# Attention with beacons and a low-rank mixer on one core: q of the third and fourth pair on SyncE's queue, w1's first quarter ahead of v's second half, U and V rounded later, and the first mixing's blocks side by side

## The chip, the cores and the metric

The kernel runs on one core of one Trainium2 chip. The metric is device time in microseconds (us) of one execution. Three runs of the kernel before gave 350.47, 351.5 and 351.79 us, so the median is 351.5 us.

## What is computed

Eight batches of eight heads attend over 576 tokens of 64 numbers. Sixteen beacon keys and values stand ahead of the tokens and are seen by every query; the tokens are causal. The attention output, as a 576 x 512 matrix x for each batch, goes through a mixer: a low-rank mixing along the tokens, and then a feed-forward layer with 2048 inner columns.

```python
scores = (q @ k_all.T) / 8            # k_all = beacons, then keys; causal on the keys
a = softmax(scores); x = a @ v_all    # 8 heads side by side: 576 x 512
u = x + ((x.T @ U) @ V).T             # U: 576 x 32, V: 32 x 576
out = u + relu(u @ w_ch1) @ w_ch2     # w_ch1: 512 x 2048, w_ch2: 2048 x 512
```

Everything comes in as float32; the kernel computes in float16 and accumulates in float32.

## The kernel before, in words

Two heads make a pair, four pairs make a batch. For each pair, k and q come in with the tokens on the partitions. TensorE transposes them (`tps`), VectorE copies the transposes to `kT` and `qT` (L310). TensorE makes the scores (`sps`, L342 and L350 for the first pairs), ScalarE takes their exponentials to `expt` (L356), and TensorE multiplies these with v (`po`, L399, one `av` unit of 15 matmuls per head). VectorE normalises the result into `xb` (L407, L408). When a batch is done its mixing runs, and then the feed-forward products: `gps` (L536, with w1) and `cps` (L562, with w2). All is written out in one order for every engine; each engine takes its instructions in that order, and the order is what the change edits.

What matters here is batch 0, the first 30 us. It is loaded through three queues.

- SyncE (SP) and ScalarE start q and k of pair 0 in float32 into `stq` and `stk` (`load_first`). After that SP loads q of pair 1 in float32 (`build_masks`, L127), released by a small write of VectorE to `stq` (L126). `regroup` (L270) then rounds such a q to float16 on VectorE, with the two heads side by side (`pr`), so that TensorE transposes it in 6 instructions (L277). A pair that is loaded as float16 is transposed in 12 instructions, head by head (L283).
- GpSimd (POOL) starts everything else, and its DMAs round to float16 on the way: k of pairs 1 and 2, q of pair 2, v's beacons, v of heads 0 to 3 (five DMAs, `v_tokens`, L220), k and q of pair 3, v of heads 4 to 7, and the first quarter of w1 (`emit_w1(0)`, L191). Then POOL rounds U (L178) and V (L179), which SP has loaded in float32 into `small` (`small_loads`), and goes on with batch 1: k and q of its heads 0 to 3, k's beacons, w1's second quarter, and so on.
- V is wanted four times, on partitions 0, 32, 64 and 96 (`Vsb`), and its last 80 columns in a block matrix (`Vend`). SP copies them there from partition 0 by seven small DMAs (L183, L184).

The first mixing, of batch 0, goes in two halves of two 128-column blocks (`first_mix`). `head` makes x.T U for two blocks: 5 matmuls, one per token tile, each with 32 output partitions and 256 columns (`qtp`, L491). VectorE rounds it to `qts` (L494). `begin` puts x transposed into PSUM (L415), `rest` adds V's product with 2 matmuls of 496 columns and 2 of 80 (L508), all four with 32 input partitions, and ScalarE and VectorE copy the sums to `uT`. The later mixings (`mix_units`, L436 and L461) do four blocks at once, each on its own 32 columns or rows of TensorE.

The order around the change is: `kt` and `qt` of pairs 2 and 3 with the scores of pairs 1 to 3 between them, `av` of pairs 0 and 1, `av` of the first head of pair 2, `head(0, 2)`, `av` of the second head, `begin`, `rest(0, 2)`, both heads of pair 3, `begin` for block 2, four products with w1 (`part(D0, 2)`, `part(D1, 2)`), `head(2, 2)`, `begin` for block 3, two more, `rest(2, 2)`, the transposes of batch 1's first pair (`qkT_of(4)`), and the feed-forward products of the first 512 rows.

Of the kernel before, what the change touches and what calls it, by code (L numbers as in the profile page):

```python
# [11 lines left out]
F32 = mybir.dt.float32  # L12
# [6 lines left out]
P = 128  # L19
# [11 lines left out]
def kernel(  # L31
# [13 lines left out]
    nc = tc.nc  # L45
    B, H, S, D = q.shape
    Nb = beacon_k.shape[2]
    DM = H * D
    R = moe_U.shape[1]
# [13 lines left out]
    NT = NC  # L63
# [58 lines left out]
    def build_masks():  # L122
        make_identity(nc, ident)
        nc.vector.memset(bigmask[:, 0, P - Nb : P], F16_MAX)
        nc.vector.tensor_copy(out=identb, in_=ident)
        nc.vector.memset(first[1][0:1, 2, 0:1], 0.0)  # L126
        token_load(nc.sync, q[0], first[1], SETS[1])  # L127
        make_upper_triangular(nc, mask, val=F16_MAX, diag=True)
        token_load(nc.gpsimd, k[0], Ls[0][0][0], SETS[1])
        nc.vector.tensor_copy(out=bigmask[:, 0, 0 : P - Nb], in_=mask[:, Nb:P])  # L130
        nc.vector.tensor_copy(out=bigmask[:, 1, :], in_=mask)
        for i in range(2):
            nc.vector.tensor_scalar(
                out=negmask[:, i, :], in0=bigmask[:, i, :], scalar1=1.0, scalar2=NEG,
                op0=ALU.is_lt, op1=ALU.mult,
            )
        prs[0] = [None, regroup(first, 0, 1, V, act_copy)]
# [26 lines left out]
    def small_loads():  # L164

        f = utp.tile([P, NT * R + S], F32, name="small", tag="ut")
        nc.vector.memset(f[0:1, 0:1], 0.0)
        uf, vf = f[:, 0 : NT * R].rearrange("p (j r) -> p j r", r=R), f[0:R, NT * R :]
        nc.sync.dma_start(out=uf[: nq[0], 0, :], in_=moe_U[0 : nq[0], :])
        nc.sync.dma_start(  # L170
            out=uf[:, 1 : NT - 1, :], in_=moe_U[q0[1] : QM, :].rearrange("(j p) r -> p j r", p=P)
        )
        nc.sync.dma_start(out=uf[:NL, NT - 1, :], in_=moe_U[QM:S, :])
        nc.sync.dma_start(out=vf, in_=moe_V)

        def cast():
            for rr, jj in ((nq[0], slice(0, 1)), (P, slice(1, NT - 1)), (NL, slice(NT - 1, NT))):
                nc.gpsimd.tensor_copy(out=Usb[:rr, jj, :], in_=uf[:rr, jj, :])  # L178
            nc.gpsimd.tensor_copy(out=Vsb[0:R, :], in_=vf)  # L179
            for cc in range(NCC):  # L180
                rs = ds(R * cc, R)
                if cc:
                    nc.sync.dma_start(out=Vsb[rs, :], in_=Vsb[0:R, :])  # L183
                nc.sync.dma_start(out=Vend[rs, cc, :], in_=Vsb[0:R, QM:S])  # L184

        return cast

# [16 lines left out]
    def token_load(eng, src, dst, hs):  # L204
        eng.dma_start(out=dst[0:TP, hs, :], in_=src[hs].rearrange("h (p j) d -> p h (j d)", j=TJ))  # L205
# [277 lines left out]
    def first_mix(xb):  # L483

        qts = outp.tile([P, DM], F16, name="qfirst", tag="ob")
        cell = {}

        def head(c0, n):
            qtp = pst([R, P * n], F32, name="qtp")
            for j in range(NT):  # L490
                nc.tensor.matmul(  # L491
                    qtp, Usb[: nq[j], j, :], xb[: nq[j], j, ds(P * c0, P * n)], start=(j == 0), stop=(j == NT - 1)
                )
            nc.vector.tensor_copy(out=qts[0:R, ds(P * c0, P * n)], in_=qtp)  # L494
            emptying(qtp)

        def begin(c0, cs, n=2):
            for cc in cs:
                cell[cc] = pst([P, QM], F32, name="ups")
                x_into(xb, cell[cc], cc, list(range(NT - 1)), 0, True)  # L500
                if cc == c0:
                    cell["end"] = pst([P, n, NL], F32, name="uend")
                x_into(xb, cell["end"][:, cc - c0, :], cc, [NT - 1], QM, cc == c0)

        def rest(c0, n, copies, end):
            for at in (0, QM):
                for i in range(n):
                    nc.tensor.matmul(  # L508
                        cell["end"][:, i, :] if at else cell[c0 + i], qts[0:R, ts(c0 + i, P)],
                        Vsb[0:R, at : S if at else QM], start=False, stop=True, skip_group_check=True,  # L510
                    )
# [161 lines left out]
    def load_first():  # L673

        kf = gtp.tile([P, 2, TJ * D], F32, name="stk", tag="gT")
        qf = gtp.tile([P, 4, TJ * D], F32, name="stq", tag="gT")
        first.extend([kf, qf])
        for src, dst in ((q[0], qf), (k[0], kf)):
            for eng, h in ((nc.sync, 0), (nc.scalar, 1)):
                token_load(eng, src, dst, slice(h, h + 1))  # L680
        Ls[0] = qk_tiles()
        key_beacons(nc.gpsimd, beacon_k[0], Ls[0][0][0], ALLH)
        nc.scalar.activation(out=warm, in_=ones, func=AF.Exp)

    def act_copy(out, in_):
        nc.scalar.activation(out=out, in_=in_, func=AF.Copy)
# [125 lines left out]
    with tc.manual_schedule(engines={ENG.PE, ENG.Activation, ENG.DVE, ENG.SP, ENG.Pool}):  # L812
        load_first()
        build_masks()
        for c in (2, 3):
            for src, dst in zip((k[0], q[0]), Ls[0][0]):
                token_load(nc.gpsimd, src, dst, SETS[c])
            if c == 2:
                v_beacon(beacon_v[0], vss[0])
                v_tokens(v[0], vss[0], HALVES[0])  # L820
        prs[0][0] = regroup(first, 0, 0, V, act_copy, beacons=False)
        idle(IDLE[0], plain)
        t0, sc = qkT_of(0), scores_of(0)
        t0[0]()
        idle(IDLE[4], ident)
        t0[1]()
        sc[0](IDLE[1], gs=[1, 0])
        prs[1] = [None, regroup(first, 1, 1, V)]
        for u in qkT_of(1):
            u()  # L830
        clear()
        cast = small_loads()
        sc[1]([3, 2], False)
        sc = scores_of(1)
        sc[0](IDLE[2])
# [19 lines left out]
        for p in range(2):  # L855
            qt, kt = qkT_of(p + 2)
            kt()
            sc[1]([3, 2], False)
            qt()
            av = av_of(p)  # L860
            av[0]()
            mask_head = sc[3]
            sc = scores_of(p + 2)
            if p:
                mask_head(0)
            sc[0](0, av[1])
            if p:
                mask_head(1)
# [252 lines left out]
```

## Time and profile before

| what | us |
|---|---|
| median of three runs | 351.5 |
| lowest and highest | 350.47, 351.79 |
| the profiled execution | 349.7 |
| its span, first to last instruction | 348.0 |
| TensorE (PE) busy in the span | 341.3 |
| VectorE, ScalarE, GpSimd busy | 189.7, 163.6, 97.8 |

The profiled execution took 1.7 us more than its span, which lies ahead of and behind the span. It is 1.8 us below the median. In the lists below, a row of the timeline gives the start in us, the time in us, the engine, the line, the operation, what is written and read with its shape, and the count of instructions that were merged; in square brackets stands the idle time of the engine before them and what ended it. A row of the chain of work gives start, time, engine, what is made and the line. A row of the DMA view gives what is written and read, the queue, the count, the KB of one DMA and the us from issue to landing. A row of the view by stretches gives the stretch, its length, the busy time of each engine, the granted clock of TensorE, the mean share of the 16 DMA engines and the GB/s that they wrote.

### The profile page before, as it was taken

The numbers are of one execution on the slowest core, as the hardware profiler recorded it, in microseconds if no ns is written. First come the engines' busy times: TensorE is split into PE (matmuls) and PEld (weight loads), VectorE is DVE, ScalarE is ACT, GpSimd is POOL, SyncE is SP. The second block draws the span as 40 slices with busy tenths as digits, with TensorE's granted clock in tenths as the row PEclk, the third lists the DMA queues.
The fourth block names the chain that finished last, engine by engine and source line by source line (L and its number), as shares of the span: only waits on it lengthen the run. The fifth ranks groups of instructions, "written<-read, shape, count | busy, mean of one in ns | idle before, by whom it ended". The sixth has DMA issues, their size and how long they took to land.

```text
span 348.0 us, 7791 instructions
## 1 busy us (share of the span) xinstructions
PE 341.3 (98%) x3084; PEld 173.2 (50%) x3084; DVE 189.7 (55%) x493; ACT 163.6 (47%) x358; POOL 97.8 (28%) x137
## 2 busy tenths in 40 slices
PE   8899999999999999999999999999999999999995
PEld 4565565455554455444554445455445444444443
DVE  6676965788875553554465556535655542323311
ACT  6957851578723664167615752494434203202300
POOL 8966714544506457303930130000000000000000
PEclk9999999999999999999999999999999999999999
DMA  9999999999999999991999697713122314013011
GB/s 166 135 186 170 169 200 171 216 148 154 128 142 145 167 133 132 154 213 14 146 139 237 64 117 123 184 38 68 62 75 47 69 62 121 2 60 106 17 66 64
DMA packets 146635, 41.88 MB, mean 120 GB/s; under 512 B 131488, under 2 KB 142080, under 8 KB 146592
## 3 DMA queue, kind: packets, MB, share of 16 engines
q0 software_dynamic: 87440, 18.18, 68.2%
q1 hardware_dynamic: 58928, 22.84, 36.0%
q8 instruction: 26, 0.43, 0.5%
q10 hardware_dynamic: 224, 0.30, 0.2%
q14 instruction: 17, 0.14, 0.1%
HBM read 37.37 MB, written 9.44 MB: 134 GB/s over the span
## 4 chain that ended last, share of the span: by engine, by line
PE 93%; POOL 2%; DMA 2%; issue 1%; DVE 1%; ACT 1%; POOLq 0%
PE gps L536 36%; PE cps L562 35%; PE po L399 8%; PE sps L384 6%; DMA st<-in_q_dram 2%; PE tps L277 1%; PE sps L350 1%; POOL vs L220 1%; PE cph L588 1%; PE qtp L436 1%; POOL st L205 1%; PE tps L283 1%; PE ups L461 1%; PE ups L415 1%; ACT expt L356 0%
## 5 line engine op out<-in xcount | busy, mean ns | idle before, releaser
L536 PE MATMUL gps<-uT,w 128*128 128x512 f16 x576 | 136.0, 379 | 0.1
L562 PE MATMUL cps<-w,gT 128*128 128x512 f16 x560 | 130.9, 379 | 0.0
L390 ACT ACTIVATE expt<-sps 128x496 f16<-128x496 f32 x192 | 82.5, 534 | 71.5 <-PE sps L384 71.5
L549 ACT ACTIVATE gT<-gps 128x512 f16<-128x512 f32 x86 | 50.9, 622 | 78.8 <-PE gps L536 78.6
L536 PEld LDWEIGHTS <-w 128*128 128x128 f16 x576 | 51.8, 98 | 58.0 <-issue 2.4
L562 PEld LDWEIGHTS <-gT 128*128 128x128 f16 x560 | 50.8, 98 | 58.9 <-issue 6.2
L551 DVE TENSOR_SCALAR gT<-gps 128x512 f16<-128x512 f32 x58 | 40.0, 690 | 41.9 <-PE gps L536 40.5
L575 DVE TENSOR_TENSOR ob<-cps,ut 128x512 f32<-128x512 f32 x31 | 21.4, 691 | 48.3 <-PE cps L562 47.5
L220 POOL DMA_DIRECT2D vs<-in_v_dram x50 | 39.6, 810 | 17.1 <-PE gps L536 5.8
L399 PEld LDWEIGHTS <-expt 128*128 128x128 f16 (+1 forms) x960 | 36.2, 98 | 12.7 <-issue 0.8
L399 PE MATMUL po<-vs,expt 128*128 128x65 f16 (+1 forms) x960 | 38.9, 194 | 0.0
L408 DVE TENSOR_TENSOR xb<-po,rec 128x320 f16<-128x320 f32 x64 | 31.5, 492 | 2.2
L326 DVE TENSOR_TENSOR expt<-expt,bigmask 128x512 f16<-128x512 f16 x58 | 24.1, 416 | 6.7 <-ACT expt L390 6.7
L356 ACT ACTIVATE expt<-sps 128x496 f16<-128x496 f32 (+2 forms) x64 | 27.1, 584 | 0.9 <-PE sps L350 0.8
L407 DVE RECIPROCAL rec<-po 128x5 f32<-128x5 f32 x64 | 12.1, 188 | 27.0 <-PE po L399 26.8
L384 PE MATMUL sps<-qT,kT 64*128 64x80 f16 (+4 forms) x288 | 23.3, 281 | 0.1
L202 POOL DMA_DIRECT2D vs<-in_beacon_v_dram x8 | 4.3, 536 | 57.8 <-PE po L399 57.7
L384 PEld LDWEIGHTS <-kT 64*128 64x128 f16 x288 | 9.9, 94 | 18.3 <-issue 14.8
L651 POOL DMA_DIRECT2D st<-in_q_dram x20 | 16.9, 863 | 6.6 <-DMA vs<-in_v_dram 2.7
L651 POOL DMA_DIRECT2D st<-in_k_dram x20 | 17.0, 883 | 3.4 <-DMA st<-in_q_dram 3.4
L448 DVE TENSOR_TENSOR uT<-ups,uT 128x496 f16<-128x496 f32 x24 | 14.5, 667 | 5.0 <-PE ups L461 5.0
L310 DVE COPY qT<-tps 128x576 f16<-128x576 f16 (+1 forms) x16 | 11.8, 736 | 4.6 <-PE tps L283 2.8
(98 smaller groups left out, 161.9 us busy)
## 6 DMA issues: line engine op xcount, KB each, us to landing
out_dram<-ob SPq DMA_DIRECT2D x35, 256.0 KB, 2.3
vs<-in_v_dram POOLq DMA_DIRECT2D x18, 128.0 KB, 6.9
w<-in_moe_w_ch_dram POOLq DMA_DIRECT2D x4, 512.0 KB, 6.1
w<-in_moe_w_ch_dram POOLq DMA_DIRECT2D x2, 1024.0 KB, 13.6
st<-in_k_dram POOLq DMA_DIRECT2D x12, 128.0 KB, 8.6
st<-in_q_dram POOLq DMA_DIRECT2D x12, 128.0 KB, 9.6
st<-in_k_dram POOLq DMA_DIRECT2D x2, 576.0 KB, 13.2
st<-in_q_dram POOLq DMA_DIRECT2D x2, 576.0 KB, 16.1
```

The lines of the kernel that those rows point to most:

```text
L220: nc.gpsimd.dma_start(out=dst[a : a + nq[j], j, :, :], in_=src[hs, ds(q0[j], nq[j]), :].rearrange("h p d -> p h d"))
L326: nc.vector.tensor_tensor(out=e4, in0=e4, in1=bigmask, op=ALU.min)
L356: nc.scalar.activation(out=ex[i][:, ds(SLOT * g, gw[g])], in_=ps[g, i][:, 0 : gw[g]], func=AF.Exp, scale=scale)
L384: nc.tensor.matmul(ps[p, g, i][:, ds(o, w)], kT[hp, c, ds(P * ch, P)], qT[hp, c, ds(qa, w)], start=True, stop=True,)
L390: nc.scalar.activation(out=at[p][3][i][:, ds(SLOT * g, gw[g])], in_=ps[p, g, i][:, 0 : gw[g]], func=AF.Exp, scale=scale)
L399: nc.tensor.matmul(po[:, j, :], ex[0 : nk[c], ds(blk[(c, j)], P)], vs[0 : nk[c], ds(c * H * E + h * E, E)], start=(c == 0), stop=(c == j),)
L408: nc.vector.tensor_tensor(out=xb[:, :, ds(h * D, D)], in0=po[:, :, 0:D], in1=r.broadcast_to([P, NT, D]), op=ALU.mult)
L536: nc.tensor.matmul(g[:, 0:n], w1[:, cc, ts(dc, P)], uT[:, cc, ds(t0, n)], start=(cc == 0), stop=(cc == NCC - 1))
L549: nc.scalar.activation(out=gT["t"][:, dc, 0:n], in_=g[:, 0:n], func=AF.Relu)
L551: nc.vector.tensor_scalar_max(out=gT["t"][:, dc, 0:n], in0=g[:, 0:n], scalar1=0.0)
L562: nc.tensor.matmul(ps[:m, :], gT["t"][:, dc, ds(P * i, m)], w2[:, dc, :], start=(dc == 0), stop=turned and dc == NDC - 1, skip_group_check ...
L651: nc.gpsimd.dma_start(out=dst[a : m[j], j, :, :], in_=src[:, ds(q0[j], nq[j]), :].rearrange("h p d -> p h d"))
```

## The change

Four things are changed, all within batch 0.

1. q of pairs 2 and 3 no longer comes through POOL's queue as float16. SP loads both in float32 into a larger `stq`, right behind q of pair 1, and VectorE rounds them (`regroup` into `pr`): pair 2 behind the clearing of `expt`, pair 3 between the k and q transposes of pair 2. TensorE transposes each with 6 instructions in place of 12.
2. On POOL, w1's first quarter is started ahead of v of heads 4 to 7. The rounding of U and V is moved behind the first three loads of batch 1.
3. U and V are loaded earlier on SP's queue (`small_loads` stands ahead of pair 1's transposes), and V comes twice, on partitions 0 and 32. POOL rounds both and writes two of Vend's four blocks; SP's copies fall from seven to four.
4. In the first mixing, `head` makes 10 matmuls of 128 columns, the two blocks on their own 32 columns of TensorE, and `rest` adds V's product from two groups of 32 rows; the 80-column products go over 64 rows with `Vend`. `begin(2, (2,))` now stands between the two heads of pair 3.

```diff
 (build_masks)
-        nc.vector.memset(first[1][0:1, 2, 0:1], 0.0)
-        token_load(nc.sync, q[0], first[1], SETS[1])
+        load_q(1)
 (small_loads)
-        uf, vf = ..., f[0:R, NT * R :]
+        uf, vf = ..., f[0 : 2 * R, NT * R :]
-        nc.sync.dma_start(out=vf, in_=moe_V)
+        for i in range(2):
+            nc.sync.dma_start(out=vf[ds(R * i, R), :], in_=moe_V)
 (cast)
-            nc.gpsimd.tensor_copy(out=Vsb[0:R, :], in_=vf)
+            nc.gpsimd.tensor_copy(out=Vsb[0 : 2 * R, :], in_=vf)
             for cc in range(NCC):
                 rs = ds(R * cc, R)
-                if cc:
+                if cc > 1:
                     nc.sync.dma_start(out=Vsb[rs, :], in_=Vsb[0:R, :])
-                nc.sync.dma_start(out=Vend[rs, cc, :], in_=Vsb[0:R, QM:S])
+                    nc.sync.dma_start(out=Vend[rs, cc, :], in_=Vsb[0:R, QM:S])
+                else:
+                    nc.gpsimd.tensor_copy(out=Vend[rs, cc, :], in_=vf[rs, QM:S])
 (first_mix, head)
-            qtp = pst([R, P * n], F32, name="qtp")
+            qtp = pst([R * n, P], F32, name="qtp")
             for j in range(NT):
-                nc.tensor.matmul(
-                    qtp, Usb[: nq[j], j, :], xb[: nq[j], j, ds(P * c0, P * n)], start=(j == 0), stop=(j == NT - 1)
-                )
+                for i in range(n):
+                    nc.tensor.matmul(
+                        qtp[ds(R * i, R), :], Usb[: nq[j], j, :], xb[: nq[j], j, ts(c0 + i, P)],
+                        start=(j == 0), stop=(j == NT - 1), skip_group_check=True, tile_position=(0, R * i),
+                    )
 (first_mix, rest)
-            for at in (0, QM):
-                for i in range(n):
-                    nc.tensor.matmul(
-                        cell["end"][:, i, :] if at else cell[c0 + i], qts[0:R, ts(c0 + i, P)],
-                        Vsb[0:R, at : S if at else QM], start=False, stop=True, skip_group_check=True,
-                    )
+            for i in range(n):
+                nc.tensor.matmul(
+                    cell[c0 + i], qts[ds(R * i, R), ts(c0, P)], Vsb[ds(R * i, R), 0:QM],
+                    start=False, stop=True, skip_group_check=True,
+                )
+            for i in range(n):
+                nc.tensor.matmul(
+                    cell["end"][:, i, :], qts[0 : R * n, ts(c0, P)], Vend[0 : R * n, i, :],
+                    start=False, stop=True, skip_group_check=True,
+                )
 (load_first)
-        qf = gtp.tile([P, 4, TJ * D], F32, name="stq", tag="gT")
+        qf = gtp.tile([P, H, TJ * D], F32, name="stq", tag="gT")
+    def load_q(*cs):
+        for c in cs:
+            nc.vector.memset(first[1][0:1, 2 * c, 0:1], 0.0)
+        for c in cs:
+            token_load(nc.sync, q[0], first[1], SETS[c])
 (the order)
         for c in (2, 3):
-            for src, dst in zip((k[0], q[0]), Ls[0][0]):
-                token_load(nc.gpsimd, src, dst, SETS[c])
+            token_load(nc.gpsimd, k[0], Ls[0][0][0], SETS[c])
 ...
         prs[0][0] = regroup(first, 0, 0, V, act_copy, beacons=False)
+        load_q(2, 3)
 ...
         sc[0](IDLE[1], gs=[1, 0])
+        cast = small_loads()
         prs[1] = [None, regroup(first, 1, 1, V)]
 ...
         clear()
-        cast = small_loads()
+        prs[2] = [None, regroup(first, 2, 1, V)]
 ...
+        emit_w1(0)
         v_tokens(v[0], vss[0], HALVES[1])
-        emit_w1(0)
-        cast()
 ...
         key_beacons(nc.gpsimd, beacon_k[1], kt, ALLH)
+        cast()
         emit_w1(1)
 ...
             kt()
+            if p == 0:
+                prs[3] = [None, regroup(first, 3, 1, V)]
             sc[1]([3, 2], False)
 ...
         av[0]()
+        begin(2, (2,))
         av[1]()
-        begin(2, (2,))
```

More of the change, by code (lines that the diff above doesn't have):

```diff
@@ L167, in small_loads @@
         nc.vector.memset(f[0:1, 0:1], 0.0)
-        uf, vf = f[:, 0 : NT * R].rearrange("p (j r) -> p j r", r=R), f[0:R, NT * R :]
+        uf, vf = f[:, 0 : NT * R].rearrange("p (j r) -> p j r", r=R), f[0 : 2 * R, NT * R :]
         nc.sync.dma_start(out=uf[: nq[0], 0, :], in_=moe_U[0 : nq[0], :])
@@ L488, in head @@
         def head(c0, n):
-            qtp = pst([R, P * n], F32, name="qtp")
+            qtp = pst([R * n, P], F32, name="qtp")
             for j in range(NT):
-                nc.tensor.matmul(
-                    qtp, Usb[: nq[j], j, :], xb[: nq[j], j, ds(P * c0, P * n)], start=(j == 0), stop=(j == NT - 1)
-                )
-            nc.vector.tensor_copy(out=qts[0:R, ds(P * c0, P * n)], in_=qtp)
+                for i in range(n):
[3 more added lines that the diff above has]
+                    )
+            nc.vector.tensor_copy(out=qts[0 : R * n, ts(c0, P)], in_=qtp)
             emptying(qtp)
```

## The prediction

> **What bounds the kernel now.** I read the page first: its span, its busy times and its slices.
>
> ```profile
> span 348.0 us, 7791 instructions
> ...
> PE 341.3 (98%) x3084; PEld 173.2 (50%) x3084; DVE 189.7 (55%) x493; ACT 163.6 (47%) x358; POOL 97.8 (28%) x137
> ...
> PE   8899999999999999999999999999999999999995
> ```
>
> TensorE is busy in 341.3 of 348.0 us, so all other engines together can give back at most 6.7 us, and the slices put that at both ends. The change edits only batch 0, the first three slices. So I read the start by stretches of 1 us, for TensorE and for the DMA engines.
>
> ```profile
> core 0: us, PE busy (x) PEld busy (x) DVE busy (x) ACT busy (x) POOL busy (x), PEclk, DMA share, GB/s
> ...
> 3.00:4.00 1.00, 1.00 (x4) 0.33 (x3) 0.67 (x5) 0.38 (x3) 1.00 (x3) 1.00 1.06 298
> ...
> 8.00:9.00 1.00, 1.00 (x17) 0.63 (x14) 1.00 (x5) 1.00 (x4) 1.00 (x2) 1.00 1.95 132
> 9.00:10.00 1.00, 1.00 (x20) 0.51 (x17) 0.40 (x11) 1.00 (x4) 1.00 (x3) 1.00 1.82 115
> 10.00:11.00 1.00, 0.78 (x16) 0.45 (x12) 0.80 (x2) 1.00 (x4) 1.00 (x2) 1.00 1.36 91
> ...
> 12.00:13.00 1.00, 0.70 (x18) 0.39 (x13) 0.96 (x3) 1.00 (x5) 1.00 (x2) 1.00 1.38 211
> ...
> 14.00:15.00 1.00, 0.90 (x20) 0.40 (x12) 0.96 (x3) 1.00 (x4) 1.00 (x4) 1.00 1.92 128
> 15.00:16.00 1.00, 0.67 (x22) 0.60 (x23) 0.51 (x3) 1.00 (x5) 0.61 (x4) 1.00 1.57 95
> 16.00:17.00 1.00, 0.70 (x16) 0.33 (x12) 0.96 (x3) 0.83 (x2) 1.00 (x2) 1.00 0.87 117
> ...
> 18.00:19.00 1.00, 1.00 (x26) 0.80 (x20) 0.97 (x5) 1.00 (x4) 1.00 (x2) 1.00 1.20 187
> ```
>
> Three things are to be seen. TensorE loses 1.25 us between 10 and 17 us (0.22 + 0.30 + 0.10 + 0.33 + 0.30) and nothing later that matters. ScalarE is full from 8 to 16. And the DMA engines are taken throughout: their share is over 1 in every row but 16:17, near 2 where v goes (132 and 115 GB/s: its rows are short), and 187 GB/s where w1 goes. The timeline names the waits.
>
> ```profile
> 6.88 9.95 ACT L356 ACTIVATE expt<-sps 128x464 f16<-128x464 f32 x24 [0.62 <-PE sps L350]
> 17.05 3.39 ACT L356 ACTIVATE expt<-sps 128x496 f16<-128x496 f32 x8 [0.23 <-PE sps L350]
> ...
> 12.69 0.58 PE L350 MATMUL sps<-qT,kT 64*128 64x496 f16 x4 [0.29 <-DVE qT L310]
> 15.34 0.45 PE L283 MATMUL tps<-ident,st 96*64 96x96 f16 x12 [0.44 <-DMA st<-in_q_dram]
> 16.64 0.58 PE L350 MATMUL sps<-qT,kT 64*128 64x496 f16 x4 [0.30 <-DVE qT L310]
> ```
>
> Only one of these waits, 0.44 us at 15.34, is for q of pair 3; the 0.29 and 0.30 are transposes that pass through VectorE. ScalarE ran 24 exponentials without a gap up to 16.83 and lacked work for 0.23 us. From 16.64 on TensorE runs without a gap, so the end moves by what TensorE gains or loses up to the feed-forward products at 26 us.
>
> **q by SP.** Two POOL issues of about 0.65 us go, and q of pair 3 lands long before 15.34. The 0.44 us wait goes, and what is late next is VectorE's copy to `qT` (the 0.30 us stays), so pair 3's scores start about 0.4 us earlier, at 16.2. ScalarE is then busy until 16.83, which caps its own gain at 0.23 us; its last eight exponentials end 0.2 us earlier, which is enough for pair 3. VectorE pays two more roundings of the kind at 6.25.
>
> ```profile
> 6.25 0.54 DVE L270 CAST pr<-stq 96x768 f16<-96x768 f32 x1
> ...
> 10.20 0.76 DVE L310 COPY kT<-tps 128x576 f16<-128x576 f16 x1 [0.79 <-PE tps L283]
> ...
> 11.88 0.76 DVE L310 COPY qT<-tps 128x576 f16<-128x576 f16 x1 [0.85 <-PE tps L283]
> ```
>
> 0.54 us fits in the 0.79 us that VectorE idles ahead of 10.20, and the second in the 0.85 us ahead of 11.88, so both cost nothing if the q's have landed by 9.6 and 11.3. If not, VectorE holds up k of pair 2 by as much. SP has nothing else to issue until the copies of V, so its queue costs nothing. The 6 transposes in place of 12 move as many numbers; the 12 took 0.45 us at 15.34, so they could give 0 to 0.2 us, and I take 0, since VectorE's copy behind them stays the limit.
>
> **w1 ahead of v.** The rows of the queue and of the landings:
>
> ```profile
> 9.82 0.67 POOL L205 DMA_DIRECT2D st<-in_q_dram  x1
> 10.46 3.63 POOL L220 DMA_DIRECT2D vs<-in_v_dram  x5
> 14.01 0.82 POOL L191 DMA_DIRECT2D w<-in_moe_w_ch_dram  x1
> ...
> 15.84 0.66 POOL L179 CAST Vsb<-small 32x576 f16<-32x576 f32 x1
> ...
> 17.12 0.68 POOL L205 DMA_DIRECT2D st<-in_q_dram  x1
> ...
> 22.49 0.75 POOL L220 DMA_DIRECT2D vs<-in_v_dram  x1 [0.87 <-DMA st<-in_k_dram]
> ```
>
> ```profile
> vs<-in_v_dram POOLq DMA_DIRECT2D x1, 40.0 KB, 4.0
> ...
> st<-in_q_dram POOLq DMA_DIRECT2D x1, 144.0 KB, 5.5
> ...
> st<-in_k_dram POOLq DMA_DIRECT2D x1, 144.0 KB, 3.7
> ...
> st<-in_q_dram POOLq DMA_DIRECT2D x1, 288.0 KB, 8.1
> ```
>
> The last of v's five DMAs was issued at 10.46 + 4 x 0.73 = 13.4 and landed 4.0 later, at 17.4. The chain of work below shows its reader, the first head of pair 2, ending at 18.75: 1.3 us of slack. After the change, w1's 512 KB (524 kB) stand ahead of it: at 187 GB/s, 2.8 us. The two q's now write four bytes per number: 295 kB at 298 GB/s is 1.0 us, against 147 kB at 211 GB/s, 0.7 us, so +0.6 us for both; V's second copy (74 kB) is +0.25 us. Together 3.65 us of transfers. What was not full gets filled: 10:11 ran at 91 GB/s and 16:17 at 117 where neighbours reach 150 to 187, which I take as 0.4 us each, 0.8 in all. If all the rest adds, v lands at 17.4 + 3.65 - 0.8 = **20.2**. The other end: SP's transfers hide wholly beside POOL's. Then POOL's queue loses the q's (1.4) and gains w1 (2.8): 17.4 + 1.4 - 0.8 = **18.0**. I take **19.6**, nearer the upper end, because the DMA share is at or above 1 in the rows where the hiding would have to happen.
>
> The rule that speaks against this move is in the Trainium skill, DMA: Bandwidth & Descriptors, "Issuing engines are not separate DMA queues": DMAs started by different engines run on the same 16 DMA engines and interleave, and only the starting engine's time is saved. By that rule v lands at the upper end, not at my value.
>
> TensorE would be at that unit 0.4 us earlier than 18.19, but its last matmul needs the last v tile, so the unit ends at 19.65 in place of 18.75: **+0.9 us**, and the 0.4 us gained by q is swallowed.
>
> **U and V later.** POOL held its DMA at 22.49 until an earlier one landed, which is the eighth before it by count. By that count k's beacons of batch 1 wait for w1's first quarter, about 2.4 us of v ahead of 19.6, so 17.2, and behind their own issue (0.68 us as at 17.12) the roundings run from 17.9. V takes the 0.66 us of 15.84. U's three pieces and Vend's two have at most a sixth of its columns; each lies between 0 and 0.66, and I take 0.2: U by 18.5, V by 19.2, Vend by 19.6. `head` runs at 19.65 and `rest` near 21, so v's lateness hides all of it. At 0.66 each U ends at 19.9 and Vend at 21.9, so up to 0.9 us would show at `rest`; without v's cover (`head` at 18.4) U would cost 0.1.
>
> **Side by side.** The chain of work has both forms, the first mixing's and the later one's.
>
> ```profile
> 18.19 0.56 PE po L399 x15
> 18.75 0.65 PE qtp L491 x5
> ...
> 20.49 0.52 PE ups L508 x2
> ...
> 25.27 0.64 PE tps L283 x24
> 25.91 3.13 PE gps L536 x14
> ...
> 49.23 0.55 PE qtp L436 x20
> ...
> 51.64 0.32 PE ups L461 x4
> ```
>
> The later form's 20 matmuls take 0.55 us, 27.5 ns each; 10 make 0.28 against 0.65, so 0.37 saved per half, 0.74 for both. Four row groups take 0.32; two lie between 0.16 and 0.32, I take 0.22 against 0.52, 0.3 saved per half. The 80-column products keep their size. What is late next is ScalarE's copy to `uT`:
>
> ```profile
> 20.83 1.06 ACT L686 ACTIVATE uT<-ups 128x496 f16<-128x496 f32 x2 [0.39 <-PE ups L508]
> 21.78 0.31 ACT L686 ACTIVATE uT<-uend 128x160 f16<-128x160 f32 x1
> ```
>
> It ends at 22.09, 1.6 us behind the start of `rest`; TensorE needed it 1.87 us behind that start (22.36), and now 1.57, so 0.03 is lost. Sum 0.74 + 0.27 + 0.3 = **1.3 us** gained. `begin` between the two heads of pair 3 changes no amount of work: 0.
>
> **The sum.** +0.9 - 1.3 = -0.4 us against the profiled execution, 349.7 to 349.3; carried to the median, 351.5 to **351.1**. It must still pass the next load: batch 1's q for pair 4, issued at 17.12 and landed 8.1 later, at 25.2. TensorE wants it behind k's half of the 0.64 us, at 25.59 - 0.4 = 25.2. No wait, and no slack.
>
> **Rivals.**
> - The transfers hide (v at 18.0). Then q's 0.4 us counts and mixing's 1.3: -1.7. But pair 4's q comes at best 0.8 us earlier, 24.4, and TensorE would be there at 23.9: 0.5 us is turned into a wait. -1.2, **350.3**. For it: the share near 2 in v's rows may be waiting, not work. Against: 187 GB/s with share 1.2 elsewhere.
> - Everything adds up (v at 20.2): +1.5 - 1.3 = +0.2, **351.7**. This is where the Trainium skill's rule leads.
> - The slower side: v comes behind the slowest DMA engine too. Pair 3's k and q are equally large and took 3.7 and 5.5 us. q's own 0.7 us of transfer is covered by its 0.67 us later issue, and U's 74 kB at v's 124 GB/s explain 0.6; 1.2 us remain for a DMA engine that lags. If that lag stands on top of 20.2, v lands at 21.4: +2.7 - 1.3 = +1.4, **352.9**. It decides from 18.75 + 1.3 = 20.05 on. For it: those two rows. Against: part of that lag is already in the 17.4.
> - The blocks do not run side by side: 10 matmuls at half of 0.65/5 each are 0.65, and two at 0.26 are 0.52, so nothing is saved: +0.9, **352.4**. The row at 49.23 speaks against it. The Trainium skill, TensorEngine Tiling (Array Packing), "Key Properties", says that a change of tiling mode drains TensorE; the 0.55 us stand between untiled products, so a drain is in them already.
>
> **How the numbers follow.** Forecast 0.36, hidden 0.18, adding 0.16, slower side 0.24, no side-by-side 0.06. Runs of before scatter by 0.6 us. The range goes from the hidden case less 0.5 us to the slower case plus 0.4: 349.8 to 353.3. Half a per cent is 1.76 us, about what a measurement of this kernel can tell from no change. Faster than 349.74 is the edge of the hidden case, if pair 4's q is no limit: 0.11. Slower than 353.26 is under half of the slower side, and what is left over: 0.19. The same: 0.70.
>
> **What would show it.** Right: no wait for q near 15, TensorE idle just ahead of the end of pair 2's first `po`, released by a v DMA that lands at 19 to 20; `qtp` of 10 matmuls near 0.28 us; first feed-forward run of 14 starting near 25.5. Wrong: that `po` without a wait (hidden case), or a landing past 20.5, or a wait of VectorE for `stq`, or a wait of `head` for U.

## The result, and the profile after

| kernel | runs | median, us | lowest to highest |
|---|---|---|---|
| before | 15 | 350.88 | 350.17 to 353.9 |
| after | 15 | 353.19 | 351.76 to 354.59 |

The ratio after to before is 1.0059, with a 95% interval of 1.0039 to 1.0079: the changed kernel is slower by 1.4 to 2.8 us. The profiled execution took 353.02 us with a span of 351.4; that of before took 349.7 with 348.0. Ratios here and below leave out runs more than 1.5% above the fastest run of the same kernel, while medians, lowest and highest count all runs.

The page of after: busy time, then TensorE's busy share and its granted clock in 40 slices.

```profile
span 351.4 us, 7794 instructions
...
PE 343.0 (98%) x3082; PEld 174.3 (50%) x3082; DVE 190.5 (54%) x497; ACT 163.9 (47%) x358; POOL 97.0 (28%) x137
...
PE   8799999999999999999999999999999999999994
...
PEclk9889999999999999999999999999999999999999
```

The second slice of TensorE fell from 8 to 7 and the third stayed at 9, and the clock shows 8 in these two, at 9 to 26 us. So the loss lies where the change was made. The largest of TensorE's waits in the first 30 us of after (in all, how often, the longest, in us) gives it a name:

```profile
PE po L401 <- DMA vs<-in_v_dram: 1.7, 3, 1.2
```

The wait for q of pair 3 (0.44 us before) is gone, and 1.7 us of waits for v are there instead. They are not the waits that the prediction looked for: they stand in pair 0, whose v is the *first* half. The timeline of TensorE, before and then after, at the first `po` unit of pair 0 (before ran it in one piece):

```profile
11.77 0.63 PE L399 MATMUL po<-vs,expt 128*128 128x65 f16 x15
```

```profile
11.94 0.22 PE L401 MATMUL po<-vs,expt 128*128 128x65 f16 x2
12.40 0.53 PE L401 MATMUL po<-vs,expt 128*128 128x65 f16 x7 [0.25 <-DMA vs<-in_v_dram]
14.09 0.35 PE L401 MATMUL po<-vs,expt 128*128 128x65 f16 x5 [1.16 <-DMA vs<-in_v_dram]
14.70 0.21 PE L401 MATMUL po<-vs,expt 80*128 80x65 f16 x1 [0.26 <-DMA vs<-in_v_dram]
```

Before, the unit ended at 12.40. After, it ends at 14.91, in four pieces, 2.5 us later. The DMA views of the two kernels, before and then after, around the issue of the last v DMA of that half (what, queue, count, KB of one, us from issue to landing), then SP's issues in after, and one of POOL's:

```profile
vs<-in_v_dram POOLq DMA_DIRECT2D x1, 40.0 KB, 2.7
```

```profile
vs<-in_v_dram POOLq DMA_DIRECT2D x1, 40.0 KB, 6.6
```

```profile
2.94 3.49 SPq L207 DMA_DIRECT2D stq<-in_q_dram  x3
6.61 0.32 SPq L168 DMA_DIRECT2D small<-in_moe_U_dram  x1
...
7.99 0.89 SPq L174 DMA_DIRECT2D small<-in_moe_V_dram  x2
```

```profile
9.31 0.79 POOL L193 DMA_DIRECT2D w<-in_moe_w_ch_dram  x1
```

POOL issues v a little earlier than before (from 4.93 in place of 5.56), yet the same 40 KB need 6.6 us in place of 2.7. What is new beside them are SP's float32 q's, then U and V, and from 9.31 on w1's first quarter. By stretches of 1 us, after (the columns are those in the prediction; the first busy time is TensorE's, and the granted clock stands third from the end):

```profile
12.00:13.00 1.00, 0.69 (x10) 0.40 (x9) 0.83 (x2) 1.00 (x4) 0.35 (x1) 1.00 1.91 159
13.00:14.00 1.00, 0.00 (x0) 0.00 (x0) 0.00 (x0) 0.76 (x2) 1.00 (x2) 1.00 1.48 178
14.00:15.00 1.00, 0.65 (x8) 0.37 (x9) 0.05 (x1) 0.00 (x0) 0.80 (x3) 0.61 1.28 213
15.00:16.00 1.00, 1.00 (x9) 0.24 (x6) 0.64 (x2) 0.52 (x2) 1.00 (x2) 0.50 1.37 188
...
20.00:21.00 1.00, 1.00 (x14) 0.54 (x11) 0.72 (x3) 0.82 (x2) 1.00 (x2) 0.50 1.27 170
21.00:22.00 1.00, 1.00 (x28) 0.78 (x26) 0.59 (x2) 1.00 (x3) 1.00 (x3) 0.98 1.15 153
```

TensorE stood from 13 to 14 us, the clock fell in the next row, and it was 0.50 in every row from 15 to 21. The chain of work of after, from the last v of pair 0 to the feed-forward products:

```profile
4.94 3.11 POOL vs L222 x4
8.04 6.61 DMA vs<-in_v_dram
...
14.70 0.21 PE po L401
...
22.31 0.40 PE qtp L494 x10
...
23.79 0.31 PE ups L511 x2
24.10 0.17 PE uend L516 x2
...
26.46 0.39 PE qtp L494 x10
...
28.14 0.64 PE tps L285 x24
```

Held against the chain of before, the lateness is +2.5 us at the end of the first `po` (14.91 against 12.40), +3.56 at the first `qtp` (22.31 against 18.75) and +2.87 at the transposes of pair 4 (28.14 against 25.27). So the wait for v's first half costs 2.5 (0.2 of it is a later start), the half clock, less what q gives, adds 1.05, and the two blocks side by side give back 0.69.

### The profile page after: what moved, and what is told of

The parts are those of the page before. It is cut to its first block, busy times and chain, and to the rows that moved or that the text cites. A ratio compares the mean times of both kernels' runs of the same rounds, so it can differ in the third digit from the quotient of the medians.

```text
span 351.4 us, 7794 instructions
## 1 busy us (share of the span) xinstructions
PE 343.0 (98%) x3082; PEld 174.3 (50%) x3082; DVE 190.5 (54%) x497; ACT 163.9 (47%) x358; POOL 97.0 (28%) x137
## 4 chain that ended last, share of the span: by engine, by line
PE 94%; DMA 2%; POOL 2%; issue 1%; ACT 1%; DVE 0%; POOLq 0%
PE gps L544 36%; PE cps L570 35%; PE po L401 9%; PE sps L386 6%; DMA vs<-in_v_dram 2%; PE sps L352 2%; PE tps L279 1%; PE cph L596 1%; POOL vs L222 1%; PE qtp L438 1%; PE tps L285 1%; PE ups L463 1%; PE ups L417 1%; ACT expt L358 0%; POOL st L207 0%
## 5 line engine op out<-in xcount | busy, mean ns | idle before, releaser
L583 DVE TENSOR_TENSOR ob<-cps,ut 128x512 f32<-128x512 f32 x31 | 21.4, 690 | 48.3 <-PE cps L570 47.6
L401 PEld LDWEIGHTS <-expt 128*128 128x128 f16 (+1 forms) x960 | 37.5, 99 | 14.9 <-issue 3.2
L222 POOL DMA_DIRECT2D vs<-in_v_dram x50 | 39.8, 808 | 13.2 <-PE gps L544 4.6
L401 PE MATMUL po<-vs,expt 128*128 128x65 f16 (+1 forms) x960 | 40.7, 196 | 1.7 <-DMA vs<-in_v_dram 1.7
L386 PEld LDWEIGHTS <-kT 64*128 64x128 f16 x288 | 9.8, 94 | 18.3 <-issue 14.8
L450 DVE TENSOR_TENSOR uT<-ups,uT 128x496 f16<-128x496 f32 x24 | 14.5, 667 | 5.0 <-PE ups L463 5.0
## 6 DMA issues: line engine op xcount, KB each, us to landing
st<-in_k_dram POOLq DMA_DIRECT2D x2, 576.0 KB, 12.3
```

Source lines behind the costliest of these rows:

```text
L222: nc.gpsimd.dma_start(out=dst[a : a + nq[j], j, :, :], in_=src[hs, ds(q0[j], nq[j]), :].rearrange("h p d -> p h d"))
L386: nc.tensor.matmul(ps[p, g, i][:, ds(o, w)], kT[hp, c, ds(P * ch, P)], qT[hp, c, ds(qa, w)], start=True, stop=True,)
L401: nc.tensor.matmul(po[:, j, :], ex[0 : nk[c], ds(blk[(c, j)], P)], vs[0 : nk[c], ds(c * H * E + h * E, E)], start=(c == 0), stop=(c == j),)
```

## The experiments

**How they are read.** Each kernel was timed beside runs of before on the same chip; before's median was 350.48, 350.81 and 350.67 us in the three batches. One profile of each serves for the mechanism, that of its first run, which can lie far from the median: mix_only's took 355.96 us, after_no_q's 352.04. The first scores started anywhere from 6.50 us (before) to 7.32 (contention_only), so places in different profiles are compared from there: "stretch" in the table is the time from the start of pair 0's first scores to the end of pair 4's 24 transposes, where the run of 14 `gps` begins (before: 25.91 - 6.50 = 19.41). The last column gives when the last of the five DMAs of each half of v landed: its issue in POOL's timeline and the time in the DMA view.

| kernel | median, us (runs) | lowest to highest | ratio to before, 95% | stretch - 19.41 | v's halves landed |
|---|---|---|---|---|---|
| before | 350.88 (15) | 350.17 to 353.9 | | 0 | 11.3, 17.4 |
| after | 353.19 (15) | 351.76 to 354.59 | 1.0039 to 1.0079 | +2.66 | 14.7, 20.8 |
| q_only | 351.51 (12) | 350.42 to 354.35 | 1.0015 to 1.0068 | -0.01 | 13.5, 17.6 |
| contention_only | 353.48 (6) | 352.77 to 354.78 | 1.0069 to 1.0113 | +2.70 | 14.8, 20.0 |
| w1_only | 356.44 (9) | 351.59 to 358.36 | 1.0050 to 1.0138 | +3.36 | 12.0, 21.5 |
| w1_warm | 352.96 (6) | 352.47 to 353.70 | 1.0052 to 1.0084 | +3.45 | 12.0, 22.0 |
| after_no_q | 354.26 (6) | 351.80 to 356.46 | 1.0074 to 1.0144 | +1.60 | 13.8, 21.5 |
| after_w1_back | 353.44 (9) | 350.87 to 355.45 | 1.0042 to 1.0107 | +1.77 | 14.9, 17.8 |
| after_uv_late | 353.53 (6) | 351.70 to 354.90 | 1.0048 to 1.0112 | +2.21 | 14.5, 21.9 |
| after_warm | 352.43 (11) | 351.74 to 354.58 | 1.0032 to 1.0080 | +1.06 | 14.5, 20.7 |
| mix_only | 352.44 (7) | 351.75 to 355.96 | 1.0031 to 1.0070 | +0.37 | 12.3, 18.3 |
| mix_good | 351.16 (12) | 350.13 to 354.96 | 1.0000 to 1.0049 | -0.24 | 12.9, 17.5 |
| mix_cast_late | 350.71 (12) | 350.25 to 351.81 | 0.9977 to 1.0015 | -1.00 | 12.0, 18.8 |

Five of these profiles have neither q by SP nor U and V early: before, w1_only, w1_warm, mix_only and mix_cast_late. In them v's first half landed between 11.3 and 12.3 us, and TensorE never waited for it. So a difference under 1 us between two landings says little.

The theory: SP's transfers take the DMA engines from v's first half, TensorE waits in pair 0, and its clock falls. The rivals: it is w1 ahead of v's second half, as the prediction had it, or the clock alone, or the mixing.

### One part at a time

**q_only.** before, with q of pairs 2 and 3 by SP:

```diff
-            for src, dst in zip((k[0], q[0]), Ls[0][0]):
-                token_load(nc.gpsimd, src, dst, SETS[c])
+            token_load(nc.gpsimd, k[0], Ls[0][0][0], SETS[c])
...
+        load_q(2, 3)
```

> Before, with q of pairs 2 and 3 by SP alone; U, V, w1 and the mixing as before. Theory A (the two float32 q's on SP's queue share the DMA engines with v's first half and go ahead of it): v's last DMA of heads 0 to 3 lands at 12.8 to 14 us instead of 11.3, the first po unit of pair 0 waits 0.7 to 1.8 us for it, and the time is 0.7 to 2.5 us longer, at the upper end if the clock falls. Rival C (w1 ahead of v is what costs): faster by 0 to 0.4 us, since only the wait for q at 15.3 goes.

From the chain of q_only, the fourth of the five DMAs of v's first half (issue, then us to landing):

```profile
7.45 5.74 DMA vs<-in_v_dram
```

It lands at 13.19, and the fifth at 13.5. In before the fifth landed at 11.3 (issued at 8.55, and 2.7 us more). So the half is 2 us later than in before, and 1.2 earlier than in after. TensorE waited 0.44 us for it, less than was expected. The time is 1.0041 times before's. So the part that was to gain 0.4 us loses something by itself; in this profile the stretch stayed the same, because the gain for pair 3 made up for the wait. The runs tell where the loss is: seven, the profiled one among them, have a granted clock of 0.996 or more over the whole run and took 350.42 to 351.87 us, and five have 0.990 to 0.993 and took 352.42 to 354.35.

**w1_only.** before, with the quarter of w1 ahead of v:

```diff
-        v_tokens(v[0], vss[0], HALVES[1])
         emit_w1(0)
+        v_tokens(v[0], vss[0], HALVES[1])
```

> Before, with w1's first quarter ahead of v's second half alone. Theory A: v's first half is untouched, so pair 0 runs as before and the clock stays; v's second half lands 2.8 us later than 17.4, near 20, so the first po unit of pair 2 ends 1 to 1.5 us later than 18.75 and the time is 0.9 to 1.5 us longer. Rival D (in the changed kernel the order of w1 and v is free because v's issue, not the engines, sets the time): no difference, 0 to 0.2 us.

The chain of w1_only, TensorE's first wait in pair 2, and two stretches:

```profile
13.31 7.86 DMA vs<-in_v_dram
...
21.20 0.59 PE po L399 x6
21.79 1.18 PE qtp L491 x5
```

```profile
19.96 0.44 PE L399 MATMUL po<-vs,expt 128*128 128x65 f16 x5 [1.49 <-ACT expt L356]
```

```profile
19.00:20.00 1.00, 0.04 (x2) 0.07 (x3) 0.53 (x2) 1.00 (x5) 1.00 (x3) 1.00 0.71 45
...
21.00:22.00 1.00, 0.89 (x10) 0.54 (x8) 0.17 (x1) 0.00 (x0) 1.00 (x2) 0.50 0.84 106
```

The fourth DMA of v's second half landed at 21.17 and the fifth at 21.5, which is the prediction's slower rival (21.4), not its 19.6. The row puts the wait of 1.49 us to ScalarE, but TensorE went on 0.14 us behind the landing of the half's first DMA (11.13 + 8.7 = 19.8), as it did in after_no_q (19.1, and 19.23), so v is the likelier end of it. TensorE stood for nearly all of 19 to 20, and the clock fell here too: the first `qtp` took 1.18 us in place of 0.65. The kernel is slower by 1.8 to 4.8 us (1.0050 to 1.0138), further than was expected. Its runs lie from 351.59 to 358.36, and in the order of their granted clock: the two at 1.00 took 351.59 and 351.65, the five at 0.984 and 0.985 took 356.44 to 358.36.

**w1_warm.** w1_only, and ten matmuls that nothing reads, ahead of pair 2's first `po`, to keep TensorE busy while it waits:

```diff
+        idle(10, ident)
         av[0]()
```

> The kernel before with w1's first quarter ahead of v's second half, as in w1_only, and ten extra matmuls of 512 columns (about 2.1 us) ahead of pair 2's first po unit, where TensorE waited for v. Theory (v's second half lands near 21.2, which costs 1.5 to 2.5 us by itself, and the granted clock's fall from 20 us on makes the rest of w1_only's loss and its scatter): the clock stays at 1.00, v lands at 21 to 21.5, the first run of 14 gps starts 1.5 to 3 us behind before's 25.91, the time is +1.5 to +3.5 over before and its spread under 3 us. Rival (the clock is beside the point): the same as w1_only, about +3.3 (351.6 to 358.4), since v's landing alone sets it.

Its chain:

```profile
13.56 8.24 DMA vs<-in_v_dram
21.84 0.44 PE po L399 x6
22.28 0.65 PE qtp L491 x5
```

The fourth and the fifth DMA of v's second half land at 21.80 and 22.0, even later, `qtp` is back at 0.65 us and the clock is 1.00 in every row from 11 to 28. The stretch did not get shorter (+3.45, where 1.5 to 3 was expected for the run of 14 `gps`), since v came later. The median is 352.96, 2.3 us over before, its runs lie within 1.2 us where w1_only's lay within 6.8, and all six have a clock of 1.00. So the scatter of w1_only went with the clock. What v's second half costs without the clock is between the 1.1 us of w1_only's two runs at 1.00 and the 2.3 us here.

### SP's transfers beside v

**after_no_q.** after, with q of pairs 2 and 3 by POOL again (the lines of q_only taken back).

> The changed kernel without its first part: q of pairs 2 and 3 by POOL as before; w1 ahead, U and V early on SP and rounded late, the mixing side by side. Theory A: v's first half lands within 1 us of 11.3 (U's and V's rows still share its time), the clock stays at 1.00, v's second half lands near 20 and costs 0.9 to 1.5, the mixing gives back 0.7: 0.2 to 0.8 us over before, so 1.5 to 2.1 under the changed kernel. Rival E (U and V, not q, hold v's first half): that half still lands near 14, and the time stays within 0.5 us of the changed kernel's.

TensorE's last wait for v in pair 0 and in pair 2 of after_no_q, and its waits for v in all:

```profile
13.81 0.19 PE L402 MATMUL po<-vs,expt 80*128 80x65 f16 x1 [0.23 <-DMA vs<-in_v_dram]
...
21.19 0.52 PE L402 MATMUL po<-vs,expt 128*128 128x65 f16 x6 [0.48 <-DMA vs<-in_v_dram]
```

```profile
PE po L402 <- DMA vs<-in_v_dram: 1.6, 5, 0.5
```

The first half still came at 13.8, 2.5 us later than in before, though q is back on POOL; TensorE waited 0.43 us for it. Most of its waits for v (1.2 of 1.6 us) are now for the second half, which landed at 21.5. The median did not fall: 354.26. The expectation had the first half within 1 us of 11.3 and the second near 20, and both were wrong. So q is enough to make v's first half late, but it is not the only thing that does: the early U and V, with w1 issued at 10.4, do it too.

**after_w1_back.** after, with w1 behind v again (the two lines of w1_only exchanged).

> The changed kernel with w1's first quarter behind v's second half again. Theory A (in the changed kernel v's first half binds, at 14.7 us, and hides v's second half, which lands at 20.9 just ahead of its use at 21.7): the wait in pair 0 and the fallen clock stay; 0 to 0.5 us faster than the changed kernel, so 352.3 to 353.2 where before is 350.5 to 350.9. Rival C (w1 is the cause): back to before or under it.

From the chain of after_w1_back:

```profile
8.13 6.76 DMA vs<-in_v_dram
```

The first half lands at 14.89, and TensorE waited 2.2 us for it in pair 0. 353.44 is after's time within the intervals. Putting either part back alone gives nothing, because each by itself makes v late enough: the two latenesses lie behind one another, and the first hides the second. In after, w1's cost was covered, since TensorE came to pair 2 late in any case (its first `po` there starts at 21.68, behind the last v at 20.8). Putting both back does help: that kernel is mix_good, below, with 351.16 us.

**after_uv_late.** after, with U and V loaded where they were:

```diff
-        cast = small_loads()
         prs[1] = [None, regroup(first, 1, 1, V)]
...
         clear()
+        cast = small_loads()
```

> The changed kernel with U and V loaded where before loads them, 3 us later. q_only, which has q alone by SP, had v's first half at 13.2 and a wait of 0.4 us, where the changed kernel has 14.7 and 1.7. Theory G (the rest of that lateness is U's and V's rows, which run beside v's): v's first half lands at 13 to 13.5, the waits for it fall under 0.8 us, the clock stays at 1.00; then v's second half is what binds, near 21, so the time stays 1 to 3 us over before. Rival H (the rest is chance or w1): the half still lands past 14.

TensorE's first and last wait for v in pair 0 of after_uv_late, and from its chain the fourth DMA of the second half:

```profile
13.24 0.25 PE L401 MATMUL po<-vs,expt 128*128 128x65 f16 x3 [0.82 <-DMA vs<-in_v_dram]
...
14.30 0.42 PE L401 MATMUL po<-vs,expt 128*128 128x65 f16 x6 [0.33 <-DMA vs<-in_v_dram]
```

```profile
14.22 7.45 DMA vs<-in_v_dram
```

Only the second DMA of the first half landed at 13.2; the fifth came at 14.5, and TensorE waited 1.35 us in pair 0 (0.82, 0.20 and 0.33). That is the rival's reading, past 14, and the theory's 13 to 13.5 is wrong: with w1 ahead of v's second half, loading U and V late does not bring the first half back. With w1 behind it, loading them early does matter: after_w1_back has 14.9, q_only 13.5. So q alone makes the half late up to 13.5, either of the other two (w1 ahead, or the early U and V) brings it to 14.5 or 14.9, and both together do no more (14.7). The parts do not add, and with one profile of each their sizes stay open. The time again stays (353.53), and v's second half is late as well: its fourth DMA lands at 21.67.

**contention_only.** before, and SP also loads q of pairs 2 and 3 in float32, which nothing reads; POOL still loads both as float16.

```diff
         prs[0][0] = regroup(first, 0, 0, V, act_copy, beacons=False)
+        load_q(2, 3)
```

> The kernel before, in which SP also loads q of pairs 2 and 3 in float32 behind q of pair 1, 295 kB that nothing reads (GpSimd still loads both as float16, and the kernel uses those). Theory (transfers on SP's queue take the DMA engines from v's short rows): v of heads 0 to 3 lands between 13 and 15 us, in place of 11.3, though nothing that is used was moved; TensorE waits for v in pair 0 for 0.5 to 2.5 us; time over before +0.7 to +3. Rival (v's first half came late in the changed kernel because of something else that the change does to the queues, such as fewer issues ahead of it): v lands within 0.5 us of 11.3 and the time is within 0.5 us of before.

The chain and two stretches of contention_only:

```profile
7.76 6.54 DMA vs<-in_v_dram
```

```profile
13.00:14.00 1.00, 0.53 (x9) 0.34 (x7) 0.47 (x1) 1.00 (x4) 1.00 (x2) 0.98 1.60 164
14.00:15.00 1.00, 0.71 (x11) 0.39 (x9) 0.00 (x0) 0.38 (x1) 1.00 (x2) 0.50 1.69 188
```

Nothing that the kernel uses was moved, no instruction of TensorE changed, and the kernel is 2.8 us slower (ratio 1.0069 to 1.0113). The fourth DMA of v's first half lands at 14.30 and the fifth at 14.8, TensorE waits 0.8 us for them, and the clock goes to 0.50. That settles that SP's transfers, and not a shorter POOL queue or the roundings on VectorE, can make all of the loss. It has POOL's 288 KB of q beside them, which after does not have, so its size isn't that of q's part.

The Trainium skill, DMA: Bandwidth & Descriptors, "Issuing engines are not separate DMA queues", has it that transfers started by different engines share the same 16 DMA engines. This run agrees: the last 40 KB of v's first half took 6.3 us beside SP's transfers, and 2.7 in before.

### The clock

**after_warm.** after, and ten matmuls that nothing reads ahead of pair 0's first `po`:

```diff
+            if p == 0:
+                idle(10, ident)
             av[0]()
```

> The changed kernel with ten more matmuls of 512 columns on no data ahead of pair 0's first po unit, so that TensorE works (2.2 us) while v is late. The output is the same. Theory I (part of the loss is the clock, which the profile shows at 0.50 from 14.5 to 21 us, behind the idle stretch): the clock stays at 1.00, the wait for v nearly disappears, and the time is 0.5 to 1.5 us shorter than the changed kernel's. Rival J (the clock costs nothing because v's second half and ScalarE set the pace there anyway): the same time within 0.3 us.

One stretch and a piece of the chain of after_warm:

```profile
13.00:14.00 1.00, 1.00 (x7) 0.47 (x5) 0.09 (x1) 1.00 (x3) 0.74 (x1) 1.00 1.29 177
```

```profile
14.52 0.46 PE po L401 x15
...
27.43 3.13 PE gps L544 x14
```

TensorE is busy from 13 to 14 and the clock is 1.00 throughout the start. The first `po` ends at 14.98, as late as in after (14.91), but from there to the run of 14 `gps` it is 12.45 us (to 27.43) in place of 13.87 (to 28.78). So in the trace the half clock is worth 1.4 us. In the times it is 0.76 (353.19 to 352.43, of different batches), and the intervals of the two ratios overlap.

The runs of each kernel, sorted by the granted clock over the whole run, say more (before has those of all three batches):

| kernel | runs at 0.995 or more | their median, us | runs below | their median, us |
|---|---|---|---|---|
| before | 57 | 350.57 | 5 | 351.98 |
| q_only | 7 | 350.98 | 5 | 353.93 |
| after_w1_back | 3 | 351.61 | 6 | 354.48 |
| after | 3 | 352.01 | 12 | 353.26 |
| after_warm | 10 | 352.38 | 1 | 354.58 |

The changed kernels do not only make v late: three of the four have a low clock in many of their runs, where before has it in 5 of 62. In after the two groups lie 1.2 us apart, close to the trace, and its runs with a high clock are still 1.4 us over before's. after_warm, in which TensorE has work while v is late, has a high clock in ten of eleven runs, and their median is within 0.4 us of after's three. Sorting runs is not a test, and three runs are few, so 1.2 us is an estimate from these rows.

### Side by side alone

**mix_only.** before with the new `small_loads`, `head` and `rest` and the moved `begin`, everything else in its old place.

> Before, with the fourth part alone: the first mixing side by side, V loaded twice and rounded with two of Vend's blocks by POOL in the old place, begin between the heads of pair 3. Theory A (all of the loss is v's first half, held up by SP's q): nothing of the loss appears here, and the mixing saves what the changed kernel's chain shows for it, 0.65 to 0.40 us for each head and 0.59 to 0.48 for each rest, 0.7 us in all: about 350.2 beside 350.9, and TensorE's clock at 1.00 throughout. Rival B (the tiled form itself costs, by switching or by the second copy of V): no gain, or up to 1 us slower.

POOL's timeline in mix_only:

```profile
17.17 0.66 POOL L180 CAST Vsb<-small 64x576 f16<-64x576 f32 x1 [0.84 <-DMA small<-in_moe_V_dram]
...
18.48 0.69 POOL L208 DMA_DIRECT2D st<-in_k_dram  x1
```

POOL waits for V's second copy, and batch 1's first load starts at 18.48 in place of 16.45; TensorE then waited 0.7 us for batch 1's beacons of k. The time is 2.0 us over before, where the expectation was a gain. The stretch is only 0.37 us longer than before's, and the profiled run is the slowest of the seven, so most of the 2.0 us lies behind the stretch and is not explained.

**mix_good.** The same, with U and V loaded early and rounded late, as in after.

> Before, with the mixing side by side, U and V loaded early on SP and rounded late; q by POOL and w1 behind v as before. Theory A (what costs is what stands ahead of v in the DMA engines; mix_only lost because POOL stood 0.84 us for V's second copy and issued batch 1's loads 2 us late): batch 1's q no longer lands late, and the mixing's 0.7 us shows: 349.5 to 350.3 beside 350.5. Rival F (U and V, early on SP, hold v's first half by themselves): pair 0's first po unit waits for v and the time is 0.5 to 2 us over before.

A wait of TensorE in mix_good:

```profile
PE tps L286 <- DMA st<-in_k_dram: 0.9, 1, 0.9
```

Loading U and V early makes k of pair 3 late by 0.9 us, and most of the gain of the mixing goes there (the next run, in which only this loading differs, has no such wait). 351.16 us is 0.35 over before, where 349.5 to 350.3 was expected. It is also after with q and w1 both put back, and 2.0 us under after: by the medians the two together make most of after's loss (the intervals of the ratios overlap, 1.0000 to 1.0049 and 1.0039 to 1.0079).

**mix_cast_late.** The same, with U and V loaded at the old place and only rounded late:

```diff
-        cast()
         Ls[1] = qk_tiles()
...
         key_beacons(nc.gpsimd, beacon_k[1], kt, ALLH)
+        cast()
```

> The kernel before with the first mixing's two blocks side by side and V twice, U and V loaded at the old place and rounded behind the first three loads of batch 1; q and w1 as before. Theory (side by side saves 0.7 us in the chain, and mix_only lost it because GpSimd waited 0.84 us for V's second copy ahead of batch 1's first loads): those loads start near 16.5 again, no wait for k of pair 3 or of pair 4, and the time is 350.0 to 350.7, that is -0.8 to -0.1 against before. Rival (V's second copy is itself 74 kB too much beside v, or rounding late makes head or rest wait for U or V): a wait of qtp or ups for U or V, or v's second half later than 17.8, and 350.8 to 352.

Chain at the start, and TensorE's waits from 55 to 110 us, of mix_cast_late:

```profile
25.69 3.13 PE gps L545 x14
```

```profile
PE sps L387 <- DVE kT L318: 0.6, 1, 0.6
PE tps L280 <- DVE gT L560: 0.4, 1, 0.4
```

No load is late now, and the stretch is 1.0 us shorter than in before. But 1.0 us of waits for VectorE stand later in the span, which before's profile does not have, and the time is 350.71 against 350.67. mix_only's profile has the first of these two waits, mix_good's has neither, so what brings them stays open; the times say that nothing is left. No version that was run beats before.

## Why the prediction was wrong

It said 351.1 us and most likely the same; the kernel takes 353.19, slower by 1.4 to 2.8 us. That the time lies in the range, at its top, is luck: the range stood on 351.5, the median of three runs of before, where fifteen give 350.88, and from there the slowest rival (+1.4) comes to 352.3. And the loss has a reason that none of the rivals had.

- **q by SP: this step failed.** "SP has nothing else to issue until the copies of V, so its queue costs nothing", and with it -0.4 us. SP did have more to issue, U and V from 6.61 on, but its issue time was indeed free; the wait at 15.34 went, and the roundings fitted, though VectorE waited 0.25 us for the second q, which landed at 11.5 and not by 11.3. The transfers were not free. The prediction counted their 295 kB each only against v's second half, which lands more than 10 us later, and never against what is in flight when they are issued: v's first half, whose landing stands in no term of the sum. In before that half had little slack (landed at 11.3, read from 11.77 on): a landing at 12.3 still made no wait (mix_only), one at 13.5 did. Measured: 13.5 with q alone, 14.7 in after, and the first `po` 2.5 us late.
- **U and V.** Rounding them later was hidden, as predicted: POOL ended it at 19.73 (predicted 19.6), and `head` and `rest` have no wait. Loading them earlier was not priced; V's second copy was, as 0.25 us for v's second half. By itself the early loading brought v's first half to 12.9 and made k of pair 3 0.9 us late (mix_good), beside q it brought the half from 13.5 to 14.9 (q_only, after_w1_back, the mixing apart), and beside q and w1 it changed little (14.5, 14.7).
- **w1 ahead of v.** The direction was right, and the size was off: 19.6 predicted, 21.5 and 22.0 measured when it is alone (w1_only, w1_warm), as in the slower rival (21.4). The 0.8 us taken off for filling rows that were not full does not show: in w1_only the rows 19:20 and 20:21, just ahead of the landing, moved 45 and 48 GB/s with a share of 0.71 and 0.77. That fits the rival's lagging engine, but no view here shows one. In after itself v landed at 20.8, past the 20.5 that the prediction set as a sign of being wrong, and cost nothing, since TensorE came to it late: the +0.9 of the sum was covered, and a larger loss stood ahead of it.
- **The clock.** No step asked what a hole in TensorE does beyond its own length. Here the clock fell behind 1.4 us of waits (0.25 and 1.16), and that cost another 1.4 us in the trace.
- **Side by side.** The blocks do run side by side: `qtp` took 0.40 and 0.39 us in place of 0.65, and the large `ups` 0.31 in place of 0.52. But 1.3 us were expected and 0.73 came. Two column groups gain less than the four of the later form, from which 0.28 was taken. And the 80-column products did not "keep their size": before they took

```profile
21.01 0.07 PE uend L508 x2
```

  and after 0.17. Per half that is 0.25 + 0.21 - 0.10 = 0.36 us, 0.73 for both with the rounding.
- **The sum.** +2.5 for v, +1.05 for the clock less q's gain, -0.69 for the mixing: 2.87 us at 28 us in the profile, of which 0.2 is a later start. The profiled execution is 3.3 us longer, so 0.5 us came after that; the medians differ by 2.3.

What stays open: how the DMA engines choose between v's rows and the others, how much each of q, w1 and the early U and V adds to the lateness of v's first half, why the clock falls in some runs of a kernel and not in others, and, beyond the estimate of 1.2 us, how much of the loss in time is the clock.

## What to carry to other kernels

Price a load that is moved to an idle queue against every transfer that is in flight when it is issued, starting with the one that has the least slack, and not only against the queue that it left or the load that the change speaks of. When two latenesses stand one behind the other, undoing either shows nothing: undo both together, try each on the kernel before as well, or add the suspected transfer to it with nothing else changed. When data come by several DMAs, go by the last of them: the landing that the chain of work shows can be an earlier one. And ask of each new wait of TensorE what the granted clock is behind it, in the profile and over every run.

## What the runs showed of the hardware

Short holes in TensorE's work were followed by half the clock. Worked out from the clocks of the rows (one at 0.61 holds 0.78 us of half clock), it lasted 6.8 us in after and in contention_only, and 3.4 us in w1_only and after_w1_back. In contention_only no row was empty ahead of it: 0.83 busy from 12 to 13 and 0.53 from 13 to 14. The Trainium skill, TensorE: Matmul & The Clock Gate, "What's actually happening", gives half the clock after one idle window of about 3.4 us. No such stretch was idle here, and the clock fell all the same, so the measurement decides. In the three rows ahead of the fall (11 to 14 us) TensorE lacked 0.86 us of work in contention_only and 1.32 us in after. But the amount alone does not settle it: after_uv_late lacked 1.35 us from 12 to 15 (0.42, 0.53 and 0.70 busy), after_no_q 1.46 us from 19 to 22 (0.35, 0.40 and 0.79), and both stayed at 1.00. What else it takes, these runs do not show.
